# Attention backward beside a gated MLP: the order of work where the MLP phase gives way to attention, and the last output tile in two parts

## The chip, the cores and the metric

The kernel runs on one core of a Trainium2 chip. Time is device time in microseconds of that core; lower is better. The core has five instruction queues: PE (TensorE, matrix products, with its weight loads shown apart as PEld), DVE (VectorE), ACT (ScalarE), POOL (GpSimd) and SP (SyncE, which here only issues DMAs). Each queue runs its instructions in the order in which they stand; between queues there are semaphores. An instruction that waits holds up everything behind it in its queue. PE writes only to PSUM, an accumulation memory of eight banks; ACT and DVE copy from there to SBUF.

## The reference

Two branches on the same 2048 x 512 input are mixed by a gate, and the kernel returns the output and the gradients of everything but one input (eight results).

```
g = sigmoid((x * gate_w).sum(-1))
a = attention(x @ wqkv) @ wo          # 32 heads of 16, causal window of 256
b = ((gate > 0) * gate * up) @ W_down # gate = x @ W_gate, up = x @ W_up, width 1376
out = g * a + (1 - g) * b
grads = vjp(out)(grad_out)            # dx, dwqkv, dwo, dW_gate, dW_up, dW_down, dgate_w
```

## The kernel before

There are three stages.

**MLP stage (0 to about 240 us).** A loop over `n` walks 44 steps (11 slices of the MLP width by 4 groups of 512 tokens, `N1 = 44`) with 8 more iterations to drain. In iteration `n` step `n` makes gate and up, step `n-2` makes dh, step `n-3` turns and stores its results by DMA (`turn_dgu`, `keep`), and step `n-6` adds its weight gradients (`weights`) into two PSUM tiles, `wg` (two banks) and `dd` (one bank). After each fourth step these are copied to SBUF by `evac`: half of `wg` on ACT, `dd` on ACT, the other half of `wg` on DVE. The weight gradients of the last slice are not made here but later, as `tail_parts`, among the attention work. All PSUM tiles of this stage (three of tag `mm`, two of tag `tr`, `wg`, `dd`: eight banks) come from one pool, `ps1`.

From iteration `N1-2` on, the same loop also runs `project_parts(*groups[0])`, the first projections of attention. This is a list of eleven parts: two halves of Q, two of dO, two of K, the transposition of K (`tr_kv`), two halves of V, the transposition of V, and `tr_rows` (a DMA transposition of Q and dO). Two parts run per iteration, three in `N1+1`, so all eleven are done before attention begins. The second half of K and of V also makes `K1` and `V1`, copies masked for odd heads (`odd`).

**Attention stage (about 240 to 690 us).** All order is written out by hand (`tc.manual_schedule`). Work goes by turns. In turn `i` the scores S of turn `i` are made (`products`, PSUM tag `S`, one buffer of two banks), ACT takes their exponential (`front`), POOL masks it (`mask`), the products D = dO V of turn `i-1` are made (tag `D`, one buffer of two banks), and DVE multiplies them (`gradp`). Then come row sums (`rowsum`, tile BA), gradients of K and V (`cd_piece`, tile CD), and `flip`: a unit's 128 x 128 blocks are transposed either on PE (8 transpositions into a `tr` tile and one copy on ACT or DVE) two turns after its scores, or by one DMA transposition on SP one turn after them (`u.dma`). Each turn has two units, `x` = 0 and 1. The unit `x` = 0 goes by DMA in nearly all turns with two blocks; the first three turns of the first chunk, `k < 3` at `c = 0`, `q = 0`, are excepted. What PE makes in spare time is the background list `bg`: projections of the next token group, then `tail_parts`. Each part has a price. Each turn a credit grows by (sum of prices left) / (turns left), and parts run while the credit covers half of the next part's price; a part that ends a PSUM tile closes it, and at most one such part runs per turn. Background tiles and flips share the two buffers of tag `tr`.

The attention pools `ps` (tags `S`, `tr`, `D`; left side of PSUM) and `psr` (BA, CD; right side) are opened when `ps1` closes. The copies out of PSUM are dealt to ACT or DVE by `share`, which keeps a running cost of each. Flipped units lie in pool `P2`, which is opened in turn 2 in place of the last MLP tiles, or, for the edge units, in one of four `wide` buffers that the stage before used for `grad_out` and for `h_end`.

**Output stage (about 690 us to the end).** Here the compiler's list scheduler orders each queue. For each of 16 token tiles `t` PE makes `bps` (MLP output, 11 products), `aps` (attention output, 4), the `wo` gradient of the tile before (`add_dwo`, 4) and `dxps` (34 products of 512 columns, lines 1118 and 1144, with the gate-weight gradient `add_dgw` between). ACT makes `da_b` = g times grad_out (line 1085, input of `add_dwo`), and from `aps` the copies `a_sb` and `ga` (1090, 1092). DVE makes `o_sb`, `amb`, `dz` and finally `dx_sb` (1150), which a DMA stores (1152).

Of the kernel before, what the change touches and what calls it, by code (L numbers as in the profile page):

```python
# [9 lines left out]
ALU = mybir.AluOpType  # L10
# [12 lines left out]
def kernel(  # L23
# [107 lines left out]
    if True:  # L131
# [4 lines left out]
        def project_parts(c, tg):  # L136
# [15 lines left out]
            def mm(nm, which, eng):  # L152
                mm_part(nm, which, range(DC // 2, DC))
                pp = acc4[nm]
                if nm in ("Q", "dO"):
                    if nm == "Q":
                        t4["z"] = pjA.tile([P, 2, TGW], BF, tag="zT", bufs=2, name="zT")
                    dst = t4["z"][:, ("Q", "dO").index(nm), :]
                else:
                    dst = pj.tile([P, TGW], BF, tag=f"{nm}0", name=f"{nm}0")[:]  # L160
                share(dst, pp[:], TGW, by=scale if nm == "Q" else None)
                t4[nm] = dst
                if nm in ("K", "V"):
                    def odd():
                        t4[f"{nm}1"] = pj.tile([P, TGW], BF, tag=f"{nm}1", name=f"{nm}1")[:]
                        share(t4[f"{nm}1"], dst, TGW, by=par[:, 1:2], sbuf=True)

                    if pools["now"][0] is pools["first"]:
                        odd()
                    else:  # L170
                        ev.setdefault(turn + 1, []).append(("dve", odd))
# [32 lines left out]
    with ExitStack() as p1, tc.manual_schedule():  # L204
        ps1 = p1.enter_context(tc.tile_pool(name="ps1", bufs=1, space=PSUM))
        ap1 = p1.enter_context(tc.tile_pool(name="acts", bufs=1))
        db_T = rows_tile("db_T")[:].rearrange("p t a n -> p (t a n)").rearrange("p (c s) -> p c s", c=DC)
# [179 lines left out]
        def weights(k):  # L387
            if k.tg == 0:
                acc["w"] = ps1.tile([P, DC, 2 * P], F32, tag="wg", bufs=1, name="wps")
                acc["d"] = ps1.tile([P, D], F32, tag="dd", bufs=1, name="dps")  # L390
            for i in range(TPG):
# [23 lines left out]
        pools["now"] = (ps1, "tr", 2)  # L415
        pools["first"] = ps1
        first = []
        turn_x(0)
        stores = {}
        for n in range(N1 + 8):  # L420
# [17 lines left out]
            for lag, end in ((3, False), (3, True)):  # L438
                if at(lag) and (at(lag).fc == FC - 1) == end:
                    turn_dgu(at(lag))  # L440
                    keep(at(lag))
            if at(6) and at(6).fc < FC - 1:
                f = weights(at(6))
                if f is not None:
                    stores[n + 1] = f
# [12 lines left out]
            if n == N1 - 2:  # L458
                first = project_parts(*groups[0])
            for _ in range({N1 + 1: 3}.get(n, 2)):  # L460
                if first:
                    first.pop(0)[1]()
            z = n - DA0 - NT - 2
# [5 lines left out]
    if True:  # L469
# [3 lines left out]
        pps = ExitStack()  # L473
        ps = pps.enter_context(tc.tile_pool(name="attps", bufs=2, space=PSUM))
        psr = p3b.enter_context(tc.tile_pool(name="attpr", bufs=1, space=PSUM, side="right"))
        pools["now"] = (ps, "tr", 2)
# [88 lines left out]
        def grad_parts(c, seam=False):  # L565
# [3 lines left out]
            def piece(part, t0, first, last):  # L569
                if first and seam:  # L570
                    tag = "SD"[part // 2]
                    if tag not in hold:
                        hold[tag] = ps.tile([P, 2, 4, P], F32, tag=tag, bufs=1, name="wps")
                    hold[part] = hold[tag][:, part % 2, 0:3, :]
                elif first:
                    hold[part] = ps.tile([P, 3, P], F32, tag="tr", bufs=2, name="wps")[:]
                wps = hold[part]
                for t in range(t0, t0 + step):
                    nc.tensor.matmul(wps, lhsT=x_r[:, t, part * P:(part + 1) * P], rhs=sts[c][:, t, 0:3, :],  # L579
                                     start=first and t == t0, stop=last and t == t0 + step - 1)  # L580
# [61 lines left out]
        for c in range(DC):  # L642
# [6 lines left out]
            for q in range(0, NT, 2):  # L649
# [5 lines left out]
                for k, (blocks, g) in enumerate(its):  # L655
                    two = []
                    for x in range(2):
                        u = Unit()
                        u.c, u.q, u.g, u.x, u.blocks, u.nb, u.at = c, q + k // 3, g + x, x, blocks, len(blocks), len(turns_)
                        u.edge = blocks[-1][1] == blocks[-1][0] - 2  # L660
                        u.dma = x == 0 and len(blocks) == 2 and (c > 0 or q > 0 or k >= 3) and (c < DC - 1 or q < NT - 2)
                        u.turn = u.at + (1 if u.dma else 2)
# [21 lines left out]
        def products(us, vs):  # L684
# [3 lines left out]
            if vs:  # L688
                vs[0].D = ps.tile([P, 2, 2, 2, P], F32, tag="D", bufs=1, name="D")
            for u in us:  # L690
# [60 lines left out]
        def place(u):  # L751
            if u.edge:
                if u.at not in wides:
                    wides[u.at] = wide("p2")
                p2 = wides[u.at][:, u.x if u.nb == 2 else 0, :, :, :]
            elif u.nb == 2 or u.x == 0:
                p2 = pools["p2"].tile([P, 2, 4, P], BF, tag="P2", bufs=14, name="p2")[:]
# [122 lines left out]
        with tc.manual_schedule():  # L880
# [3 lines left out]
            closed = {}  # L884
            bg = []
            jobs = tail_parts()
            ready = []
# [23 lines left out]
            def lead(us):  # L911
                c, qs, ks = us[0].c, [b[0] for b in us[0].blocks], [b[1] for b in us[0].blocks]
                return "dO" in proj.get((c, max(qs) // TPG), {}) and "V1" in proj.get((c, max(ks) // TPG), {})

# [15 lines left out]
            while turn < NI + 3 or ev or cdq or bg or sums:  # L930
# [41 lines left out]
                if vs:  # L972
                    gradp(vs)
                if turn == 2:
                    fend.close()
# [70 lines left out]
    with ExitStack() as p56:  # L1046
        x_r5 = x_r

        with ExitStack() as p6:
# [18 lines left out]
            for g in range(NG):  # L1068
# [3 lines left out]
                for tl in range(GT):  # L1072
# [11 lines left out]
                    da_b = t6.tile([P, D], BF, tag="da_b")  # L1084
                    nc.scalar.mul(da_b[:], go_g[:, tl, :], g_all[:, t:t + 1])
                    pending_wo.append((t, o_g[:, tl, :, :], da_b))
# [4 lines left out]
                    ga = t6.tile([P, D], F32, tag="ga")  # L1091
                    nc.scalar.mul(ga[:], aps[:], g_all[:, t:t + 1])
                    o_sb = t6.tile([P, D], BF, tag="o_sb")
                    nc.vector.scalar_tensor_tensor(out=o_sb[:], in0=bps[:], scalar=omg_all[:, t:t + 1], in1=ga[:],
# [17 lines left out]
                    dxps = ps6.tile([P, D], F32, tag="dxps", bufs=1)  # L1112
                    nmm = 2 * FC + C3
                    i = 0

                    def gate_up(src, wt, i):
                        for fc in range(FC):
                            nc.tensor.matmul(dxps[:], lhsT=col(src, fc, lsl), rhs=W6[(wt, fc)],  # L1118
                                             start=(i + fc == 0), stop=(i + fc == nmm - 1))
                        return i + FC  # L1120

                    i = gate_up(dgT_g, "Wg", i)
                    if t > 0:
                        i = gate_up(duT_g, "Wu", i)

# [4 lines left out]

                    if pending_dgw is not None:
                        add_dgw(*pending_dgw)
                    pending_dgw = (t, dz_bf)
                    for cc in range(C3):
                        if t == NT - 1 and cc == 3:
                            add_dgw(t, dz_bf)
                            nc.scalar.copy(dgw_sb[:, 0:DC], dgw_ps[:])
                        if t == NT - 1 and cc == C3 - 4:
                            dgw_t = psa.tile([P, P], BF, tag="aps", bufs=1, name="dgw_t")
# [3 lines left out]
                            nc.sync.dma_start(out_7.rearrange("(c p) -> c p", p=P), dgw_row[:])  # L1143
                        nc.tensor.matmul(dxps[:], lhsT=T_g[:, 4 * (cc % DC) + cc // DC, lsl], rhs=W6[("wqkv", cc)],  # L1144
                                         start=(i == 0), stop=(i == nmm - 1))
                        i += 1
                    if t == 0:
                        gate_up(duT_g, "Wu", i)
                    dx_sb = t6.tile([P, D], BF, tag="dx_sb")
                    nc.vector.scalar_tensor_tensor(out=dx_sb[:], in0=S2["gw"][:], scalar=dz[:, 2:3], in1=dxps[:],  # L1150
                                                   op0=ALU.mult, op1=ALU.add)
                    (nc.sync if t == NT - 1 else nc.gpsimd).dma_start(dx_d[tsl, :], dx_sb[:])

# [29 lines left out]
```

## Time and profile before

| | us |
|---|---|
| median of 3 runs | 882.41 (881.83 to 884.45) |
| the profiled execution | 882.34 |
| its span, first to last instruction | 880.6 |
| PE busy | 855.1 (97%) |
| DVE, POOL, ACT busy | 507.2, 478.4, 395.0 |

A row of a timeline has the start in us, the length in us, the engine, the line of the kernel, the operation, output and input tiles, shapes and a count. The bracket at its end is the time for which the engine stood idle before it, and what released it. The ends of matrix products are modelled, and each overlaps the next; the time from start to start of successive products is what PE needs for them. A row of the windows view gives for a stretch of the span its length and the busy time of PE, then (with the number of instructions) of the other engines asked for, the granted clock of TensorE, the busy share of the DMA engines and GB/s.

### The profile page before, as it was taken

What the parts mean: (1) busy time and instruction counts of PE and PEld (TensorE: products, weight loads), DVE (VectorE), ACT (ScalarE), POOL (GpSimd) and SP (SyncE); (2) the same over time, 40 slices, a digit from 0 to 9 for tenths busy, and PEclk for the clock granted to TensorE, in tenths of its full rate; (3) what the DMA queues carried; (4) which work ended last, traced back from release to release, by engine and by line L of the source; (5) the groups of instructions that cost most, each with busy time, mean ns of one, the idle gap of its engine ahead of it and who ended that gap; (6) DMA issues with size and microseconds to landing.
All of it is one profiled execution on the core that took longest, in us unless ns stands there. A gap on an engine that the chain in (4) does not pass through costs nothing. (4 is left out here: it accounts for less than half of the span.)

```text
span 880.6 us, 29350 instructions
## 1 busy us (share of the span) xinstructions
PE 855.1 (97%) x12545; PEld 555.7 (63%) x12545; DVE 507.2 (58%) x763; ACT 395.0 (45%) x569; POOL 478.4 (54%) x887
## 2 busy tenths in 40 slices
PE   7999999999989999999999999999999999999998
PEld 4556665666557877777777767777778544444443
DVE  4544542332367888887888778887786132222222
ACT  5522222222366676765667656676554211111111
POOL 1644444444347787876778767787678222222111
PEclk9999999999999999999999999999999999999999
DMA  9999999999757999799998989999999999778731
GB/s 274 237 187 194 205 211 209 203 210 204 174 103 121 155 154 153 110 140 160 179 142 112 137 161 183 158 142 152 182 216 188 243 282 235 182 183 178 185 83 49
DMA packets 440876, 153.56 MB, mean 174 GB/s; under 512 B 369352, under 2 KB 438312, under 8 KB 440744
## 3 DMA queue, kind: packets, MB, share of 16 engines
q1 hardware_dynamic: 437144, 145.51, 88.5%
q0 software_dynamic: 2016, 5.64, 1.9%
q8 instruction: 98, 1.61, 0.8%
q10 hardware_dynamic: 1584, 0.53, 0.2%
q14 instruction: 34, 0.28, 0.1%
HBM read 32.15 MB, written 36.24 MB: 78 GB/s over the span
## 5 line engine op out<-in xcount | busy, mean ns | idle before, releaser
L725 DVE TENSOR_TENSOR PP<-PP,D 128x1024 bf16<-128x1024 bf16 (+1 forms) x184 | 219.0, 1190 | 56.1 <-POOL PP L718 21.6
L708 ACT ACTIVATE PP<-S 128x1024 bf16<-128x1024 f32 (+1 forms) x184 | 185.2, 1007 | 95.9 <-PE D L675 47.3
L718 POOL TENSOR_SCALAR_AFFINE_SELECT PP<-PP 128x512 bf16<-128x512 bf16 (+1 forms) x188 | 143.3, 763 | 80.2 <-ACT PP L708 77.6
L74 DVE COPY p<-pt 128x1024 bf16<-128x1024 bf16 x164 | 112.3, 685 | 10.9 <-PE pt L779 10.9
L355 POOL TENSOR_TENSOR hgu<-rg,upm 128x512 bf16<-128x512 bf16 x44 | 50.8, 1155 | 120.7 <-DVE upm L353 103.5
L779 PE MATMUL pt<-ident,PP 128*128 128x128 bf16 x1512 | 113.9, 218 | 0.1
L742 PE MATMUL BA<-KV,PP 128*128 128x33 bf16 x1440 | 106.6, 180 | 2.1 <-ACT BAs L72 1.6
L742 PEld LDWEIGHTS <-PP 128*128 128x128 bf16 x1440 | 85.7, 96 | 31.2 <-issue 11.9
L744 PE MATMUL BA<-KV,PP 128*128 128x17 bf16 x1440 | 102.4, 170 | 0.0
L395 PE MATMUL wps<-hgu_r,x_r 128*128 128x256 bf16 x640 | 96.0, 273 | 0.0
L493 PE MATMUL CD<-rq,p 128*128 128x32 bf16 x1440 | 94.8, 176 | 0.0
L496 PE MATMUL CD<-rq,p 128*128 128x16 bf16 x1440 | 93.6, 169 | 0.0
L744 PEld LDWEIGHTS <-PP 128*128 128x128 bf16 x1440 | 84.6, 96 | 10.7 <-issue 7.3
L779 PEld LDWEIGHTS <-PP 128*128 128x128 bf16 x1512 | 86.1, 97 | 0.2 <-issue 0.2
L493 PEld LDWEIGHTS <-p 128*128 128x128 bf16 x1440 | 80.7, 95 | 0.3
L496 PEld LDWEIGHTS <-p 128*128 128x128 bf16 x1440 | 80.5, 96 | 0.3
L395 PEld LDWEIGHTS <-x_r 128*128 128x128 bf16 x640 | 62.6, 98 | 28.6
L675 PE MATMUL S<-zT,K 32*128 32x128 bf16 (+3 forms) x1056 | 77.2, 238 | 1.5 <-ACT PP L708 0.7
L675 PE MATMUL D<-zT,V 32*128 32x128 bf16 (+3 forms) x1056 | 72.2, 237 | 4.6 <-DVE PP L725 4.0
L353 DVE SCALAR_TENSOR_TENSOR upm<-rg,ups 128x512 bf16<-128x512 bf16 x44 | 30.2, 687 | 80.3 <-PE ups L340 58.8
L1090 ACT COPY a_sb<-aps 128x512 f32<-128x512 f32 x16 | 9.3, 583 | 131.0 <-issue 106.5
L363 POOL TENSOR_TENSOR hgu<-dh_sb,rg 128x512 bf16<-128x512 bf16 x44 | 58.7, 1334 | 9.0 <-ACT dh_sb L361 9.0
(147 smaller groups left out, 1514.3 us busy)
## 6 DMA issues: line engine op xcount, KB each, us to landing
hgu_d<-hgu SPq DMA_DIRECT2D x44, 384.0 KB, 3.4
dqkvo_d<-rows_st SPq DMA_DIRECT2D x14, 512.0 KB, 3.8
duT_g<-hgu_d SPq DMA_DIRECT2D x8, 640.0 KB, 5.3
gt<-hgu_d SPq DMA_DIRECT2D x7, 640.0 KB, 5.6
dgT_g<-hgu_d SPq DMA_DIRECT2D x7, 640.0 KB, 5.0
p<-PP SPq DMA_TRANSPOSE x171, 4.0
out_dram<-wst SPq DMA_DIRECT2D x20, 128.0 KB, 2.9
go_in<-in_grad_out_dram SPq DMA_DIRECT2D x4, 512.0 KB, 9.4
```

What stands on the lines that cost most here:

```text
L74: nc.vector.tensor_copy(out, in_)
L363: nc.gpsimd.tensor_tensor(out=k.hgu[:, 2, :], in0=dh_sb[:], in1=k.rg[:], op=ALU.mult)
L395: nc.tensor.matmul(acc["w"][:, c, :], lhsT=x_r[:, t, c * P:(c + 1) * P], rhs=k.dgu_r[:, :, i, :], start=(go_ and c % 2 == 0), stop=no_, sk ...
L493: nc.tensor.matmul(cd[0][:, h, :], lhsT=p2[:, 0, pr, :], rhs=rq[:, h, 0:2 * Dh], start=cd[1], stop=True, skip_group_check=True)
L496: nc.tensor.matmul(cd[0][:, h, 0:Dh], lhsT=p2[:, 1, pr, :], rhs=rq[:, h, 2 * Dh:3 * Dh], start=False, stop=True, skip_group_check=True)
L675: nc.tensor.matmul(dst, lhsT=proj[(u.c, kb // TPG)][nm + ("", "1")[par]][rows[par], (kb % TPG) * P:(kb % TPG + 1) * P], rhs=proj[(u.c, qb ...
L708: nc.scalar.activation(two[:].rearrange("p x a b q -> p x a (b q)")[:, :, 0, 0:n], flat(us[0].S[:], n), ACT.Exp)
L718: nc.gpsimd.affine_select(out=out, in_=out, compare_op=ALU.is_ge, fill=0.0, base=0 if up else -1, pattern=[[0, 2], [0, b1 - b0], [1 if up ...
L725: nc.vector.tensor_tensor(out=v(1), in0=v(0), in1=flat(vs[0].D[:], n), op=ALU.mult)
L742: nc.tensor.matmul(BA[:, h, 0:33], lhsT=u.PP[:, 0, 2 * i + pr, :], rhs=kv[:, kb % TPG, h, 1:34], start=(first and pr == 0), stop=True, ski ...
L744: nc.tensor.matmul(BA[:, h, 33:50], lhsT=u.PP[:, 1, 2 * i + pr, :], rhs=kv[:, kb % TPG, h, 0:17], start=False, stop=True, skip_group_check ...
L779: nc.tensor.transpose(pt[:, a, b if u.nb == 2 else 2 * u.x + b, :], u.PP[:, a, b, :], ident[:])
```

## The change

1. The MLP stage's `wg` and `dd` go to a pool of their own, `psw`, on the right side of PSUM. `D` goes to a pool of its own, `psd`, beside `ps`.
2. In the MLP loop, iteration `N1-2`, `N1-1` and `N1` run the two parts of Q, dO and K; `N1` also runs `tr_rows`, and `N1+1` runs K's transposition, ahead of `weights`. V's three parts are kept in a list `behind`. Turn 0 of attention starts when `K1` is there: it makes the first scores, then V's two parts, then two parts from the background list, apart from those that the credit allows. Turn 1 makes V's transposition behind its scores, products and `gradp`.
3. The units `x` = 0 of the first two turns are flipped by DMA too, into a `wide` buffer, since `P2` isn't open yet.
4. `da_b` is written behind `a_sb` and `ga`, except in the last tile.
5. In the last tile `dxps` is made in two parts: 34 products of 384 columns, then 34 of 128 columns into a tile of tag `bps`; each part has its own DVE operation and store. The work on the gate-weight gradient stays in the first part.

```diff
+        psw = p1.enter_context(tc.tile_pool(name="psw", bufs=1, space=PSUM, side="right"))
...
-                acc["w"] = ps1.tile([P, DC, 2 * P], F32, tag="wg", bufs=1, name="wps")
-                acc["d"] = ps1.tile([P, D], F32, tag="dd", bufs=1, name="dps")
+                acc["w"] = psw.tile([P, DC, 2 * P], F32, tag="wg", bufs=1, name="wps")
+                acc["d"] = psw.tile([P, D], F32, tag="dd", bufs=1, name="dps")
...
+            if n == N1 + 1:
+                first.pop(0)[1]()
             if at(6) and at(6).fc < FC - 1:
                 f = weights(at(6))
...
-            for _ in range({N1 + 1: 3}.get(n, 2)):
-                if first:
-                    first.pop(0)[1]()
+            for _ in range({N1 - 2: 2, N1 - 1: 2, N1: 2}.get(n, 0)):
+                first.pop(0)[1]()
+            if n == N1:
+                first.pop()[1]()
...
+        psd = pps.enter_context(tc.tile_pool(name="attpd", bufs=1, space=PSUM))
...
-                        u.dma = x == 0 and len(blocks) == 2 and (c > 0 or q > 0 or k >= 3) and (c < DC - 1 or q < NT - 2)
+                        u.dma = x == 0 and len(blocks) == 2 and (c < DC - 1 or q < NT - 2)
...
-                vs[0].D = ps.tile([P, 2, 2, 2, P], F32, tag="D", bufs=1, name="D")
+                vs[0].D = psd.tile([P, 2, 2, 2, P], F32, tag="D", bufs=1, name="D")
...
+            elif u.at < 2 and u.x == 0:
+                if "p2" not in wides:
+                    wides["p2"] = wide("p2")
+                p2 = wides["p2"][:, u.at, :, :, :]
...
+            behind = [f[1] for f in first]
...
-                return "dO" in proj.get((c, max(qs) // TPG), {}) and "V1" in proj.get((c, max(ks) // TPG), {})
+                return "dO" in proj.get((c, max(qs) // TPG), {}) and ("K1" if turn == 0 else "V1") in proj.get((c, max(ks) // TPG), {})
...
                 if vs:
                     gradp(vs)
+                if turn == 0:
+                    behind.pop(0)()
+                    behind.pop(0)()
+                    background()
+                    background()
+                elif behind:
+                    behind.pop(0)()
...
-                    nc.scalar.mul(da_b[:], go_g[:, tl, :], g_all[:, t:t + 1])
+                    if t == NT - 1:
+                        nc.scalar.mul(da_b[:], go_g[:, tl, :], g_all[:, t:t + 1])
...
                     nc.scalar.mul(ga[:], aps[:], g_all[:, t:t + 1])
+                    if t < NT - 1:
+                        nc.scalar.mul(da_b[:], go_g[:, tl, :], g_all[:, t:t + 1])
...
+                    def dx_part(dxps, n0, n1, pending):
+                        count = [0]
+
+                        def product(w, key):
+                            nc.tensor.matmul(dxps[:, n0:n1], lhsT=w, rhs=W6[key][:, n0:n1], start=(count[0] == 0), stop=(count[0] == nmm - 1))
+                            count[0] += 1
...
+                        nc.vector.scalar_tensor_tensor(out=dx_sb[:, n0:n1], in0=S2["gw"][:, n0:n1], scalar=dz[:, 2:3], in1=dxps[:, n0:n1],
+                                                       op0=ALU.mult, op1=ALU.add)
+                        (nc.sync if t == NT - 1 else nc.gpsimd).dma_start(dx_d[tsl, n0:n1], dx_sb[:, n0:n1])
+
                     dx_sb = t6.tile([P, D], BF, tag="dx_sb")
...
+                    cut = D if t < NT - 1 else D - P
+                    dx_part(ps6.tile([P, D], F32, tag="dxps", bufs=1, name="dxps"), 0, cut, pending_dgw)
+                    if cut < D:
+                        dx_part(psa.tile([P, D], F32, tag="bps", bufs=1, name="dxps_end"), cut, D, None)
+                    pending_dgw = (t, dz_bf)
```

More of the change, by code (lines that the diff above doesn't have):

```diff
@@ L166, in odd @@
                         share(t4[f"{nm}1"], dst, TGW, by=par[:, 1:2], sbuf=True)
-                    if pools["now"][0] is pools["first"]:
+                    if (c, tg) == groups[0]:
                         odd()
@@ L415 @@
         pools["now"] = (ps1, "tr", 2)
-        pools["first"] = ps1
         first = []
@@ L572, in piece @@
                     if tag not in hold:
-                        hold[tag] = ps.tile([P, 2, 4, P], F32, tag=tag, bufs=1, name="wps")
+                        hold[tag] = (ps if tag == "S" else psd).tile([P, 2, 4, P], F32, tag=tag, bufs=1, name="wps")
                     hold[part] = hold[tag][:, part % 2, 0:3, :]
@@ L1111 @@
                             nc.sync.dma_start(out_3[c * P:(c + 1) * P, :], ws[:])
-                    dxps = ps6.tile([P, D], F32, tag="dxps", bufs=1)
                     nmm = 2 * FC + C3
[L1114 to L1124, printed above, removed]
                     def add_dgw(t_, dz_):
@@ L1129, in add_dgw, with gate_col_grad @@
                                              start=(t_ == 0 and c == 0), stop=(t_ == NT - 1), skip_group_check=True)
[L1131 to L1135, printed above, removed]
+                    def gate_col_grad(cc):
+                        if cc == 3:
                             add_dgw(t, dz_bf)
                             nc.scalar.copy(dgw_sb[:, 0:DC], dgw_ps[:])
-                        if t == NT - 1 and cc == C3 - 4:
+                        if cc == C3 - 4:
                             dgw_t = psa.tile([P, P], BF, tag="aps", bufs=1, name="dgw_t")
@@ L1143 @@
                             nc.sync.dma_start(out_7.rearrange("(c p) -> c p", p=P), dgw_row[:])
[L1144 to L1148, printed above, removed]
-                    dx_sb = t6.tile([P, D], BF, tag="dx_sb")
-                    nc.vector.scalar_tensor_tensor(out=dx_sb[:], in0=S2["gw"][:], scalar=dz[:, 2:3], in1=dxps[:],
-                                                   op0=ALU.mult, op1=ALU.add)
@@ L1152, with gate_up @@
-                    (nc.sync if t == NT - 1 else nc.gpsimd).dma_start(dx_d[tsl, :], dx_sb[:])
+                    def dx_part(dxps, n0, n1, pending):
[3 more added lines that the diff above has]
+                            count[0] += 1
+                        def gate_up(src, wt):
+                            for fc in range(FC):
+                                product(col(src, fc, lsl), (wt, fc))
+                        gate_up(dgT_g, "Wg")
+                        if t > 0:
+                            gate_up(duT_g, "Wu")
+                        if pending is not None:
+                            add_dgw(*pending)
+                        for cc in range(C3):
+                            if t == NT - 1 and n0 == 0:
+                                gate_col_grad(cc)
+                            product(T_g[:, 4 * (cc % DC) + cc // DC, lsl], ("wqkv", cc))
+                        if t == 0:
+                            gate_up(duT_g, "Wu")
+                        nc.vector.scalar_tensor_tensor(out=dx_sb[:, n0:n1], in0=S2["gw"][:, n0:n1], scalar=dz[:, 2:3], in1=dxps[:, n0:n1],
+                                                       op0=ALU.mult, op1=ALU.add)
+                        (nc.sync if t == NT - 1 else nc.gpsimd).dma_start(dx_d[tsl, n0:n1], dx_sb[:, n0:n1])
```

## The prediction

> **What bounds the kernel now.** After the page's shares I read the view of busy time by stretches of the span, with the seam between MLP and attention cut out, and then the timelines there, PE's first.
>
> ```profile
> 300.00:400.00 100.00, 97.11 (x2361) 74.19 (x2360) 85.07 (x123) 67.97 (x93) 79.76 (x180) 1.00 0.98 142
> ...
> 712.00:870.00 158.00, 158.00 (x780) 72.33 (x778) 42.27 (x94) 25.98 (x44) 30.34 (x40) 1.00 0.71 173
> ...
> sum 20.00, PE 15.98; mean PE 2.66
> ```
>
> PE is the bound: it works 97.11 of 100 us in attention and 158 of 158 in the output stage. The last row is the sum over 237 to 257 us, the seam: PE works 15.98 of 20.00 us and idles 4.02. Only there can work be put into holes. What is won there should stay won: attention runs PE at 97% behind it, and every later event hangs on the turns.
>
> ```profile
> 239.67 0.39 PE L187 MATMUL ptp<-ident,K 128*128 128x128 bf16 x4
> 239.90 1.03 PE L149 MATMUL pp<-x,p 128*128 128x512 bf16 x4
> 241.60 0.40 PE L187 MATMUL ptp<-ident,V 128*128 128x128 bf16 x4 [0.68 <-ACT V L72]
> 242.51 0.39 PE L675 MATMUL S<-zT,K 16*128 16x256 bf16 x4 [0.52 <-DVE KV L74]
> ...
> 244.14 0.28 PE L675 MATMUL S<-zT,K 16*128 16x256 bf16 x2 [0.27 <-ACT PP L708]
> ...
> 246.12 0.28 PE L675 MATMUL D<-zT,V 16*128 16x256 bf16 x2 [0.24 <-DVE PP L725]
> ...
> 246.67 1.05 PE L779 MATMUL pt<-ident,PP 128*128 128x128 bf16 x16
> 248.50 1.02 PE L149 MATMUL pp<-x,p 128*128 128x512 bf16 x4 [0.78 <-DVE p L74]
> ...
> 251.78 0.38 PE L187 MATMUL ptp<-ident,K 128*128 128x128 bf16 x4 [0.73 <-DVE p L74]
> ...
> 255.90 0.28 PE L675 MATMUL S<-zT,K 16*128 16x256 bf16 x2 [0.28 <-ACT PP L708]
> 256.57 0.23 PE L675 MATMUL D<-zT,V 16*128 16x128 bf16 x2 [0.38 <-DVE PP L725]
> ```
>
> The brackets name the holes. V's transposition waits 0.68 for ACT's copy of V; the first scores wait 0.52 for the copy of that transposition, the last reader of `ps1`; the flips of turns 2 and 3 take 16 transpositions each (246.67, and the same ahead of 251.78), so both `tr` buffers, and the next projection waits 0.78 and 0.73 for one. The brackets sum to 3.88, nearly the 4.02.
>
> **The change, part by part.** *Scores ahead of V, pools of their own.* What stands on the other queues:
>
> ```profile
> 240.14 0.59 ACT L72 CAST dst<-dps 128x512 bf16<-128x512 f32 x1
> 240.96 0.59 ACT L72 CAST V<-pp 128x512 bf16<-128x512 f32 x1 [0.23 <-PE pp L149]
> 243.07 1.02 ACT L708 ACTIVATE PP<-S 128x1024 bf16<-128x1024 f32 x1 [1.52 <-PE S L675]
> ```
> ```profile
> 240.88 0.51 DVE L90 TENSOR_SCALAR KV<-ptp 128x512 bf16<-128x512 bf16 x1
> ...
> 244.85 1.22 DVE L725 TENSOR_TENSOR PP<-PP,D 128x1024 bf16<-128x1024 bf16 x1 [2.39 <-POOL PP L718]
> ...
> 247.76 0.69 DVE L74 COPY p<-pt 128x1024 bf16<-128x1024 bf16 x1
> ```
> ```profile
> 237.97 1.39 POOL L363 TENSOR_TENSOR hgu<-dh_sb,rg 128x512 bf16<-128x512 bf16 x1 [2.95 <-ACT dh_sb L361]
> ...
> 239.36 0.31 POOL L183 MEMSET KV<- 128x32 bf16 x1
> 244.17 0.65 POOL L718 TENSOR_SCALAR_AFFINE_SELECT PP<-PP 128x512 bf16<-128x512 bf16 x1 [4.49 <-ACT PP L708]
> ```
>
> K's transposition moves ahead of the last weight products, which then end at 239.90 (0.23 later, as the K row and the next start). The first scores can start there instead of at 242.51, since S no longer shares a pool with the copies of `wg` and `dd`. But K's copy into KV must be done first, as the last reader of `ps1`. It writes the tile of POOL's memset, which ends at 239.67 behind L363; if the copy waits for that, it ends at 239.67 + 0.51 and the scores start at 240.2. So 239.9 to 240.2; I take 240.2, because DVE's copy is the kind of wait that the bracket of 0.52 shows. ACT then takes the exponential behind `dst` at about 240.9 instead of 243.07. Behind the scores PE has V, Q of the next group, and dO by the credit (at turn 0 about 9.0 of prices over 11 turns, 0.82, against 0.43 for the first half of a projection): three projections of 0.86 (four products of 512 columns; 0.216 each, worked out with the tail), where it stood still. That third one needs the `tr` buffer of V, so ACT's copy of V, which now stands behind the exponential: 240.9 + 0.92 + 0.59 = 242.4, when PE, at 242.2, waits 0.2. Turn 1 starts near 243.3 instead of 244.14, with dO (0.86) done ahead: 1.7 us ahead. Queued behind the waiting things: dO's copy stands on DVE ahead of the first `gradp`, which starts at 244.1 instead of 244.85, so turn 2 waits for its end at 245.3 (0.3), and turn 3 for the second one (K's copy 0.69, then 1.22, done at 247.4) about 0.8; turn 5 waits 0.6 in the same way. New holes: 0.3 + 0.2 + 0.3 + 0.8 + 0.6 = 2.2, and by the same rows no more than the old 4.02.
>
> *First flips by DMA.* Eight of the 16 transpositions in each of turns 2 and 3 leave PE, and with them one copy per turn leaves DVE or ACT. How long 16 take, and eight products of 384 columns, is in the chain, where it runs without a break; the third row is of the 13 flips by DMA between 250 and 285.
>
> ```profile
> 669.90 0.91 PE pt L779 x16
> 676.92 1.30 PE wps L579 x8
> ```
> ```profile
> DMA to landing us min/median/max: 3.0/3.8/4.9
> ```
>
> Sixteen take 0.91 on PE: that is removed. With 8 per turn one `tr` buffer stays free, so the two holes of 0.78 and 0.73 go, by what the turns with one such flip show, none of which is named in the brackets between 252 and 255; they are among the 4.02. The two DMAs stand on SP, issued from 245.3 and 247.5. Flips of this kind land within 4.9 us, by 252.4. SP's stores of the MLP stage lie ahead of them, and `tr_rows` leaves that place for one ahead of the last `turn_dgu`; it delays that by its issue of about 1.3 us (the row of it below), which only the background work from 255 on needs. The readers of the flips come in turn 6.
>
> ```profile
> 243.23 1.28 SPq L175 DMA_TRANSPOSE rows<-zT  x1
> ...
> 257.12 0.18 PE L493 MATMUL CD<-rq,p 128*128 128x32 bf16 x1
> ```
>
> Before, they start at 257.12; some 3 us earlier that is 254, still 1.7 behind the landing. Cost 0; if the cover went, at most 0.5 by a late landing in a busy stretch.
>
> *Sum at the seam.* Holes of 4.02 plus 0.91 of work removed, less the 2.2 of new holes: 2.7. The ends are 4.02 + 0.91 = 4.9 (no new hole) and 0.4 (new holes as long as the old ones plus the 0.5). I take 2.8, a little above the sum, since two of the new holes overlap copies that the shorter flips bring forward.
>
> *`da_b` behind `a_sb` and `ga`.*
>
> ```profile
> 857.48 0.72 ACT L1085 ACTIVATE da_b<-gt,g_all 128x512 bf16<-128x512 bf16 x1
> 867.95 0.59 ACT L1090 COPY a_sb<-aps 128x512 f32<-128x512 f32 x1 [9.75 <-issue]
> ```
>
> ACT is idle 9.75 us per tile, and the scheduler already puts the next tile's `da_b` behind this tile's `ga`. Its reader, `add_dwo`, comes a tile later. I take 0; the ends are a gain of some tenths in the first tile, where ACT's `da_b` waits for the load of `grad_out`, and the loss of the second rival.
>
> *Last `dx` in two parts.*
>
> ```profile
> 869.60 4.75 PE dxps L1118 x22
> ...
> 877.23 0.75 DVE dx_sb L1150
> ```
> ```profile
> 705.82 0.15 DVE L1102 TENSOR_TENSOR dz<-g_all,omg_all 128x1 f32<-128x1 f32 x1
> ```
> ```profile
> out_dram<-dx_sb SPq DMA_DIRECT2D x1, 128.0 KB, 1.7
> ```
> ```profile
> out_dram<-wst SPq DMA_DIRECT2D x2, 128.0 KB, 2.8
> out_dram<-dst SPq DMA_DIRECT2D x1, 128.0 KB, 2.6
> ```
>
> 34 products of 512 columns at 0.216 (4.75 / 22) take 7.3. Of 384 columns they take 0.1625 (1.30 / 8), of 128 columns 0.057 (0.91 / 16): 34 x 0.2195 = 7.46, so PE ends 0.1 later. DVE's last operation falls from 0.75 for 512 columns towards 0.15 for one: 0.15 + 0.60/4 = 0.30, so 0.45 less. The last store has 32 KB instead of 128; how much of its 1.7 is fixed no row shows, so 0 to 0.4, and I take 0.2. The first part's DVE operation (about 0.6) and store lie beside the second part's 1.94 of PE. Sum 0.45 + 0.2 - 0.1 = 0.55, ends 0.1 and 0.8. The Trainium skill, "DMA: Bandwidth & Descriptors", Specifications, speaks against this: it gives 512 B as the least transfer at full rate, with a read-modify-write below, and the second store has rows of 256 B. In this trace the stores of `wst`, with such rows, take 2.8 us to land and that of `dst`, of as many bytes in 1 KB rows, 2.6, so the trace agrees in direction and shows little of it; by the page the 0.2 would go and the sum here be about 0.35.
>
> ```profile
> span 880.6 us, 29350 instructions
> ```
>
> **Total.** 2.8 + 0.55 = 3.3, of the profiled execution's 882.34 (span 880.6 and 1.7 around it). That lies within 0.1 of the median, so I carry it over: 882.4 - 3.3 = 879.1.
>
> **The rivals.** *A: the new holes cost more.* DVE sets the pace of turns 1 to 5: `gradp` 1.22, a flip copy 0.69 and a projection's cast 0.69 stand in one queue, and turns are closer. If two more waits as long as those it removes appear (0.78 + 0.73), the gain is 3.3 - 1.5 = 1.8: 880.6. For it speaks that D waits for DVE twice already; against it that DVE has 2.39 of idle time ahead of its first `gradp`.
>
> *B: slower, by `da_b`.* If the scheduler places `add_dwo` of a tile where its `da_b` isn't done, PE waits for 0.72 in each of 15 tiles: 10.8 us, so 882.4 - 3.3 + 10.8 = 889.9. It decides the sign from 0.22 per tile on. Against it: the 9.75 of idle time on ACT; for it: PE has no slack in that stage (158 of 158), so any wait there counts fifteen times.
>
> *C: won at the seam and lost again before the output stage.*
>
> ```profile
> 690.00:707.00 17.00, 14.97 (x70) 1.00 1.09 240
> ```
> ```profile
> 700.08 0.52 POOL L527 MEMSET d<- 32x512 bf16 x1 [11.79 <-DMA d<-in_B_W_up_dram]
> ```
>
> There PE idles 2 us, and its release comes from POOL's memset, which waits for a DMA, with DMA engines full (1.09). If that DMA doesn't come earlier, the 2.8 is lost and the tail's 0.55 stays: 881.9. Against it: the loads are issued by events of the last turns, so they move along.
>
> **How the numbers follow.** The forecast 0.57, A 0.19, C 0.10, B or another slowdown 0.14. A change under 0.3% (2.65 us) can hardly be told from none here. Faster by more means below 879.76: most of the forecast's own range, 877.0 to 880.2, and a small part of A: 0.56. Within: C, most of A: 0.30. Slower: 0.14. The low end is the seam's 4.9 plus the tail's 0.55, 877.0. The high end must pass A and C and leave out B: 882.8, no gain at all and 0.4 for the scatter of the runs.
>
> **What would show it.** Right: in the profile after, scores at 240 us, idle PE of about 2 in the 20 us from 237, 16 fewer L779, the last DVE operation near 0.3 us, and no idle PE from tile to tile in the output stage. Wrong: a bracket at the first scores beyond 1 us; D waiting for `gradp` in most turns to 257; CD waiting for the DMA flips; the first output tile starting no earlier than 686 to 690; an idle time at `wo_ps`.

## The result, and the profile after

| | before | after |
|---|---|---|
| median, us | 882.93 (7 runs, 881.83 to 884.45) | 879.87 (7 runs, 878.61 to 881.28) |
| ratio | | 0.9964, 95% interval 0.9952 to 0.9975 |
| the profiled execution | 882.34 | 881.28 |
| its span | 880.6 | 879.6 |

The changed kernel is 3.06 us faster; 3.3 were forecast, and a time of 879.1. The two profiled executions differ by only 1.06 us, and the profile after is of the slowest of its seven runs. So a reader who takes the difference of the two spans for the effect of the change is misled by 2 us. Where those 2 us went can be found in the trace.

PE's timeline of the changed kernel at the seam (row sums and a few products left out):

```profile
236.20 0.39 PE L187 MATMUL ptp<-ident,K 128*128 128x128 bf16 x4
...
239.13 0.39 PE L679 MATMUL S<-zT,K 16*128 16x256 bf16 x4
239.46 1.90 PE L149 MATMUL pp<-x,p 128*128 128x512 bf16 x8
241.55 1.02 PE L149 MATMUL pp<-d,p 128*128 128x512 bf16 x4 [0.19 <-ACT V L72]
242.51 0.28 PE L679 MATMUL S<-zT,K 16*128 16x256 bf16 x2
...
245.03 0.61 PE L787 MATMUL pt<-ident,PP 128*128 128x128 bf16 x8
245.47 0.39 PE L187 MATMUL ptp<-ident,K 128*128 128x128 bf16 x4
245.79 0.28 PE L679 MATMUL S<-zT,K 16*128 16x256 bf16 x2
246.68 0.23 PE L679 MATMUL D<-zT,V 16*128 16x128 bf16 x2 [0.61 <-DVE PP L729]
...
250.78 0.28 PE L679 MATMUL D<-zT,V 16*128 16x256 bf16 x2 [0.29 <-DVE PP L729]
...
260.23 0.82 PE L624 MATMUL wps<-dgu_end,x_r 128*128 128x192 bf16 x8 [0.58 <-DVE p L74]
```

The first scores follow the last weight products without a bracket; V, Q and dO stand in a row behind them; eight transpositions are followed by K's transposition without a wait. Holes of 0.19, 0.61 and 0.29 are left, and one of 0.58 at 260.23. The whole execution was already 0.86 us earlier at the end of the MLP stage, which belongs to its first 35 us and not to the change (over all profiles this mark lies between 227.69 and 229.57, in old and new kernels mixed), so times of the two profiles are better compared as distances between marks. Four marks that each kernel has once: the start of the last `hgu` on POOL (end of the MLP stage), of the fourth and the last `rinv` on DVE (attention under way, attention's end), and of the fourth `dz` on DVE (output stage under way). In the changed kernel:

```profile
227.69 1.15 POOL L356 TENSOR_TENSOR hgu<-rg,upm 128x512 bf16<-128x512 bf16 x1 [3.62 <-DVE upm L354]
```
```profile
270.73 0.19 DVE L803 RECIPROCAL rinv<-BAs 128x8 f32<-128x8 f32 x1
...
673.86 0.19 DVE L803 RECIPROCAL rinv<-BAs 128x8 f32<-128x8 f32 x1
...
732.68 0.69 DVE L1120 TENSOR_REDUCE dz<-amb 128x1 f32<-128x512 f32 x1 [1.46 <-POOL amb L1118]
```

and in the kernel before:

```profile
228.55 1.15 POOL L355 TENSOR_TENSOR hgu<-rg,upm 128x512 bf16<-128x512 bf16 x1 [3.62 <-DVE upm L353]
```
```profile
274.69 0.19 DVE L795 RECIPROCAL rinv<-BAs 128x8 f32<-128x8 f32 x1
...
677.56 0.19 DVE L795 RECIPROCAL rinv<-BAs 128x8 f32<-128x8 f32 x1
...
733.50 0.69 DVE L1101 TENSOR_REDUCE dz<-amb 128x1 f32<-128x512 f32 x1 [1.46 <-POOL amb L1099]
```

The seam (first to second mark) takes 43.04 instead of 46.14 us: 3.10 won. Attention takes 403.13 instead of 402.87. The start of the output stage takes 58.82 instead of 55.94: 2.88 lost in this execution. The view of waits of the changed kernel between 660 and 714 us (who waited for whom; us in total, times, longest) names the place:

```profile
PE dxps L1153 <- DMA d<-in_B_W_up_dram: 1.9, 1, 1.9
PE dxps L1153 <- POOL d L531: 0.9, 1, 0.9
PE dxps L1153 <- DVE dx_sb L1171: 0.2, 1, 0.2
```

PE waits for a load of W_up, then for the memset behind it, and TensorE's clock drops as well (below). Rival C of the prediction had named this place. Whether the change causes it is what the experiments had to decide.

### The profile page after: what moved, and what is told of

The parts are those of the page before. It is cut to its first block, busy times and chain, and to the rows that moved or that the text cites. A ratio compares the mean times of both kernels' runs of the same rounds, so it can differ in the third digit from the quotient of the medians.

```text
span 879.6 us, 29392 instructions
## 1 busy us (share of the span) xinstructions
PE 856.6 (97%) x12563; PEld 557.2 (63%) x12563; DVE 507.9 (58%) x764; ACT 393.5 (45%) x567; POOL 478.5 (54%) x887
```

## The experiments

The same four marks in every profile, in us between them, with the lead at the seam over 46.14:

| kernel | seam | lead | attention | output start |
|---|---|---|---|---|
| before | 46.14 | | 402.87 | 55.94 |
| last dx in two parts alone | 46.14 | 0 | 402.95 | 58.60 |
| `da_b` moved alone | 46.15 | 0 | 403.07 | 57.27 |
| before, late memset | 46.64 | | 403.48 | 55.89 |
| changed, first profile | 43.04 | 3.10 | 403.13 | 58.82 |
| changed, second | 43.05 | 3.09 | 403.19 | 56.43 |
| changed, third | 43.04 | 3.10 | 403.10 | 56.97 |
| parts 1 to 3 alone | 43.04 | 3.10 | 403.20 | 57.10 |
| without first flips by DMA | 44.62 | 1.52 | 403.11 | 56.35 |
| without own pools | 43.99 | 2.15 | 403.08 | 57.38 |
| changed, late memset | 43.04 | 3.10 | 403.31 | 55.56 |
| the same again | 43.04 | 3.10 | 403.10 | 56.97 |
| early W_up | 43.03 | 3.11 | 410.89 | 54.14 |
| early W_up, late memset | 43.04 | 3.10 | 407.23 | 54.84 |

Apart from one outlier (46.64) the seam repeats within 0.02 us, so one profile is enough there for a difference well above that outlier's 0.5. In the outlier TensorE's clock dropped at the seam (the last section has the row); its edit stands 440 us later. The start of the output stage doesn't repeat: kernels with the old seam and the memset where it was show 55.94 to 58.60 (mean 57.27), those with the new seam 56.35 to 58.82 (mean 57.18).

**The changed kernel again.** No edit.

> The changed kernel once more, unchanged. Theory S (the seam's gain of 3.1 us reaches the last tiles; what its first profile lost between 682 and 712 us is chance of one execution): the median is 2.6 to 3.6 us under before, and this profile keeps 2 us or more of the lead of 3.7 to 3.9 us behind 712. Theory C (the load of W_up's transposition does not come earlier, so the lead is always lost there): again under 1 us of lead behind 712, and the median gain stays near 1 us.

Median 880.23 against 883.38: ratio 0.9962 (0.9945 to 0.9978). The lead at the seam is 3.09. Behind 712 us this execution stands 2.9 ahead of the one before, 0.6 of which it had from its first 35 us. A third set, taken later beside another kernel:

> The changed kernel, for the comparison with the late memset. Theory S: 2.6 to 3.6 us under the kernel before, for the third time; in its profile the lead at 275 us beyond that at the end of the MLP stage is 3.1 again, and what is left of it at 712 us lies between 0 and 3.

Ratio 0.9949 (0.9935 to 0.9962), lead 3.10, output start 56.97. By the medians that is 4.1 us, more than the 2.6 to 3.6 expected: the changed kernel is where it was (879.63), and the kernel before is slower in this set (883.75). Theory C falls: the lead is not always lost, and the old kernels show the same scatter.

**The parts alone.** The seam alone keeps the old `da_b` and

```diff
-                    cut = D if t < NT - 1 else D - P
+                    cut = D
```

> Parts 1 to 3 of the change (scores ahead, pools, first flips by DMA); da_b and the last dx as before. Theory S: the seam carries the gain, 2.4 to 3.3 us faster than before, lead of about 3.1 us (beyond any difference at the start) from 270 us on. Rival T (the tail carries it): under 1 us.

Ratio 0.9971 (0.9959 to 0.9984), 2.6 us of 883.4 (3.1 by the medians), lead 3.10: the seam carries nearly all.

The other two are the kernel before with that part of the change's diff alone.

> Part 5 alone (last dx in two parts). By the prediction 0.55 us faster (0.1 to 0.8): last DVE operation 0.35 instead of 0.75, PE 0.1 later, store 0.2 shorter. By the first profile of the changed kernel 0.2. Rival T: over 1.5 us.

> Part 4 alone (da_b behind a_sb and ga). Theory: no difference, within 0.5 us of before, since ACT idles 9.7 us per tile. Rival B: 0.7 us per tile lost at the wo products, 10 us slower. Rival G: a_sb and ga of tile 0 no longer wait for the load of grad_out, some tenths faster.

The dx in two parts alone gives 1.0002 (0.9990 to 1.0015), `da_b` alone 0.9996 (0.9983 to 1.0008): neither can be told from nothing. For the last tile the profiles say more than the medians. DVE's last operations and the end, in the profile of the two-part dx alone:

```profile
877.53 0.61 DVE L1152 SCALAR_TENSOR_TENSOR dx_sb<-gw_b,dz,dxps 128x384 bf16<-128x384 bf16 x1 [1.90 <-PE dxps L1134]
879.43 0.35 DVE L1152 SCALAR_TENSOR_TENSOR dx_sb<-gw_b,dz,dxps_end 128x128 bf16<-128x128 bf16 x1 [1.29 <-PE dxps_end L1134]
```
```profile
out_dram<-dx_sb SPq DMA_DIRECT2D x1, 96.0 KB, 1.6
out_dram<-dx_sb SPq DMA_DIRECT2D x1, 32.0 KB, 1.4
```

From the last tile's `dz` to the end of the span, four profiles with one part take 8.63 to 8.96 (mean 8.72), ten with two parts 8.35 to 8.52 (mean 8.43): 0.29 won, or 0.21 without the one of 8.96. DVE's operation fell from 0.75 to 0.35 and PE's products took 0.09 more, as forecast. The last store lands 1.4 us after its issue here, and 1.4 or 1.5 in the other nine, instead of 1.7 in the four with the whole store. But the span ends no sooner for it: from the end of DVE's operation to the end of the span it is 2.62, 2.62, 2.65 and 2.96 in one part and 2.65 to 2.82 in two. What lies between the landing and the end of the span is in no view.

**What carries the seam.** The two kernels of this part ran once each, so only their profiles are used. First the old condition for the flips again:

```diff
-                        u.dma = x == 0 and len(blocks) == 2 and (c < DC - 1 or q < NT - 2)
+                        u.dma = x == 0 and len(blocks) == 2 and (c > 0 or q > 0 or k >= 3) and (c < DC - 1 or q < NT - 2)
```

> The changed kernel with part 3 undone: the units x = 0 of the first two turns are flipped on PE again. Measured as the lead over the kernel before at the row sums (rinv), less the difference already there at the end of the MLP stage. By the prediction part 3 brings 0.91 of PE work and the two waits of 0.78 and 0.73, so the lead at 270 us falls from 3.1 to about 0.7. Rival: with scores and projections spread otherwise the waits for tr do not come back, and only the 0.9 goes: a lead of 2.2.

The waits of PE between 236 and 262 us in that kernel:

```profile
PE ptp L187 <- ACT p L72: 0.7, 1, 0.7
PE D L679 <- DVE PP L729: 0.4, 1, 0.4
PE pp L149 <- DVE p L74: 0.3, 1, 0.3
PE pp L149 <- ACT V L72: 0.2, 1, 0.2
```

The lead is 1.52, between the two expectations: the flips are worth 1.58. The waits for a `tr` buffer do come back, as 0.70 and 0.34 instead of 0.78 and 0.73; with the 0.91 of transpositions that would be 1.95, and the waits for `gradp` become 0.46 shorter (0.44 instead of 0.61 and 0.29), which leaves 1.5.

Then the pools, both put back at once:

```diff
-                acc["w"] = psw.tile([P, DC, 2 * P], F32, tag="wg", bufs=1, name="wps")
-                acc["d"] = psw.tile([P, D], F32, tag="dd", bufs=1, name="dps")
+                acc["w"] = ps1.tile([P, DC, 2 * P], F32, tag="wg", bufs=1, name="wps")
+                acc["d"] = ps1.tile([P, D], F32, tag="dd", bufs=1, name="dps")
...
-                vs[0].D = psd.tile([P, 2, 2, 2, P], F32, tag="D", bufs=1, name="D")
+                vs[0].D = ps.tile([P, 2, 2, 2, P], F32, tag="D", bufs=1, name="D")
```

> The changed kernel with the PSUM pools put back (wg and dd in ps1, D in ps), order and flips as changed. By the prediction the first scores then wait for the copies of wg and dd (ACT and DVE, done about 1.4 us after the last weight product), so S starts 1.2 to 1.5 us later and the lead at 270 us is about 1.8 instead of 3.1. Rival: the order alone carries it, the lead stays at 2.9 or more.

```profile
240.63 0.39 PE L677 MATMUL S<-zT,K 16*128 16x256 bf16 x4 [1.19 <-DVE wst L74]
```

The scores wait 1.19 for DVE's copy of the weight gradients, as expected; 0.95 of it is left in the lead, since the 0.2 of waiting for V's copy then goes. So of the 3.10 the flips carry about half (1.58), the pools a third (0.95); what is left by subtraction, 0.57, would be the order's if the parts simply added up; it wasn't run alone.

**The start of the output stage.** The order of POOL's queue there, in the second profile of the changed kernel:

```profile
697.17 0.52 POOL L531 MEMSET d<- 32x512 bf16 x1 [12.26 <-DMA d<-in_B_W_up_dram]
697.63 2.92 POOL L590 DMA_DIRECT2D out_dram<-ws  x4
700.05 1.05 POOL L1115 DMA_DIRECT2D out_dram<-o_sb  x1
700.62 1.67 POOL L1118 TENSOR_TENSOR amb<-amb,go_g 128x512 f32<-128x512 f32 x1
```

A memset of half a microsecond stands 12.26 us at the head of the queue, waiting for a load; behind it four stores whose data has long been there, and behind these `amb`, on which PE's second `dxps` hangs. So:

```diff
-            clear("Wu")
             for f in S2["grads"]:
                 store = f()
                 if store is not None:
                     store()
+            clear("Wu")
```

> The changed kernel with the memset of W_up's last rows on POOL moved behind the stores of the last wqkv gradients. Theory C1 (POOL's queue behind the memset is what PE waits for at the second output tile): the four stores, 2.9 us, leave the path, amb of tile 0 comes 2.9 us earlier after the memset, and the median falls by up to 2 us (the wait at the second dx). Rival C2 (the DMA of W_up's rows itself is the wait): PE still waits for it in the first dx, and the median stays within 0.7 us of the changed kernel.

Five runs gave 878.67, ratio 0.9940 (0.9928 to 0.9953). PE's waits between 676 and 714 us, in its profile:

```profile
PE dxps L1153 <- POOL d L531: 1.0, 1, 1.0
PE dxps L1153 <- DMA d<-in_B_W_up_dram: 0.4, 1, 0.4
```

The wait of 1.9 for the second dx (`dxps` for DVE's `dx_sb`), which the profile before and the second and third of the changed kernel have, is gone, as C1 says; what is left is the load itself, as C2 says. Once more, beside the changed kernel on the same chip:

> The changed kernel with the late memset again, beside the changed kernel itself in the next run on the same chip. If its gain of the first time (five runs: 878.67 against some 880.2) is real, 1.2 to 2.2 us under the changed kernel again. If it was the luck of those five runs, as the gain of only 0.4 us in the kernel before suggests, within 0.7 us of it.

Median 878.28 against 879.63, ratios 0.9942 (0.9926 to 0.9958) and 0.9949 (0.9935 to 0.9962) to the kernel before. The intervals overlap: faster than the changed kernel by 0.6 us (ratios) or 1.4 (medians) in this set, not proved. In this profile, of the slowest of the six runs, the wait for `dx_sb` is gone too, but PE waits 2.8 us in all for the load and the memset of W_up, and the output stage's start takes as long as in the changed kernel beside it (56.97). The kernel before with the same edit:

> The kernel before with only the memset of W_up's last rows moved behind the stores. If the wait behind the memset is there in both kernels (1.91 us in the profile before), this is 1 to 2 us faster than before, and the gain adds to that of the change. Rival: the change made that wait, by coming to it earlier, and here the time stays within 0.5 us of before.

Ratio 0.9986 (0.9973 to 0.9999), which is 1.2 us, but 0.4 by the medians: its twelve runs fall into two groups, five from 879.9 to 881.5 and seven from 883.0 to 885.7. The wait of 1.9 is in the old kernel too and goes here as well; whether that is worth 0.4 or 1.2 us these runs don't settle. This edit on the changed kernel gave the lowest medians of all.

Taking the load out of the way altogether, into the last chunk of attention, where late loads then go every second turn from token tile 8 on instead of 12:

```diff
+                14: turns("Wu", B_W_up, 4, 8, "x2") + turns("Wu", B_W_up, 8, 12, "d2") + [lambda: clear("Wu")],
...
-            for f in turns("Wu", B_W_up, 4, 8, "x2") + turns("Wu", B_W_up, 8, 12, "d2"):
-                f()
-            clear("Wu")
...
-                if late and (late[0] is not load_wo or turn > NI) and (not us or turn % (4 if us[0].c == DC - 1 and us[0].q < 12 else 2) == 1):
+                if late and (late[0] is not load_wo or turn > NI) and (not us or turn % (4 if us[0].c == DC - 1 and us[0].q < 8 else 2) == 1):
```

> The changed kernel with W_up's last four transposing loads and their memset moved from the start of the output stage into the list of late loads of the last chunk of attention, where their buffers are free; late loads then go every second turn from token tile 8 on instead of 12. If the load of W_up is what the output stage's start waits for (C2), the waits between 682 and 712 us go and the kernel is 1.5 to 4 us faster than the changed one, with less scatter. Rival: the DMA engines are full in the last attention turns too, flips land late there, and what is won at 700 is lost before 680 (lead at 677 us falls under 3).

Ratio 1.0001 (0.9991 to 1.0011): the whole gain is gone. The output start is the shortest of all (54.14), and attention takes 7.8 us more. POOL between 640 and 684 us, and then the waits of all engines in that stretch:

```profile
648.68 1.09 POOL L723 TENSOR_SCALAR_AFFINE_SELECT PP<-PP 128x1024 bf16<-128x1024 bf16 x1 [1.69 <-ACT PP L713]
656.16 0.51 POOL L531 MEMSET d<- 32x512 bf16 x1 [6.38 <-DMA d<-in_B_W_up_dram]
```
```profile
DVE PP L730 <- POOL PP L723: 7.5, 5, 6.1
POOL d L531 <- DMA d<-in_B_W_up_dram: 6.4, 1, 6.4
PE D L680 <- DVE PP L730: 5.8, 1, 5.8
```

It is the same memset again: it waits 6.38 us for its load, the masks stand behind it, `gradp` behind the masks, PE behind `gradp`. With the memset moved behind the stores:

> As the kernel with the early loads of W_up, but its memset on POOL stands behind the stores of the last wqkv gradients, not among the masks of attention. Theory M (the loss between 640 and 680 us there was the memset: it waited 6.4 us for its DMA at the head of POOL's queue, masks and gradp behind it): no wait of 5.8 us, a lead of about 3.1 at 677 us kept to 712, and a time of 877 to 878.5, up to 1.4 us under the kernel with the late memset alone, since the wait for W_up in the first dx goes too. Rival D (the DMA engines are what is short): flips land late between 640 and 680, CD or gradp wait, and the time is that of the kernel with the late memset or more.

The wait of 5.8 is gone, as theory M says. But the time is 882.26, ratio 0.9994 (0.9983 to 1.0006): at the `rinv` of 657.71 this execution is still 3.2 us ahead of the one before (0.6 of it from the first 35 us), and at the last one, 678.23, it is 0.7 behind. A wait that this profile adds there:

```profile
ACT PP L713 <- DMA p<-PP: 5.4, 4, 2.0
```

ACT's exponential waits four times for a buffer whose flip by DMA hasn't landed. The changed kernel's profiles have no such wait, so rival D holds in that the flips are late, and about 4 us are lost for 2 won. Its cause is not shown: the DMA engines' mean share from 660 to 684 us is 1.10 here and 1.07 in the first profile of the changed kernel, the moved loads also stand in SP's queue between the flips, and the kernel before with the late memset, which moved no load, has two such waits (2.4 us) at 665 to 669.

## Why the prediction was right

- **The total** was forecast at 3.3 and measured at 3.06 (879.1 against 879.87). From the table and the tail: 3.10 at the seam, less 0.17 in attention (mean of the three old kernels without the late memset 402.96, of the six new ones 403.13), 0.1 at the output start (means, far inside its scatter), 0.2 to 0.3 in the last tile: 3.2 to 3.3. The seam gave 0.3 more than forecast and the last tile about 0.3 less; that the total was met is partly luck. Of the 0.8 between 879.1 and 879.87, 0.5 is the starting point: 882.4 was the median of three runs, that of seven is 882.93.
- **The seam** was forecast at 2.8 and measured at 3.10. PE from the first mark to the second, before and then changed:

```profile
228.55:274.69 46.14, 41.93 (x634) 1.00 0.67 124
```
```profile
227.69:270.73 43.04, 40.91 (x617) 1.00 0.81 142
```

  PE idles 2.13 us instead of 4.21 and works 1.02 us less: 2.08 + 1.02 = 3.10. So the forecast's terms come out near in sum (4.02 of holes removed, 0.91 of work, 2.2 of new holes), but not each new hole in its place. In the 20 us from 237 the changed PE idles 1.35 us, where about 2 were forecast (first row below). Of the five new holes, the first scores' 0.3 did not come: DVE's copy into KV ran at 237.41, ahead of POOL's memset of that tile at 238.51 (the other rows), so the dependency that I held possible isn't there. dO's 0.2 came as 0.19; turn 2's 0.3 left no bracket; turn 3's 0.8 came as 0.61 and turn 5's 0.6 as 0.29. A hole of 0.58 at 260.23 I had not seen: one background part is done earlier, and the next needs a `tr` buffer behind DVE's flip copy; I take that from the order, no run tests it.

```profile
237.00:257.00 20.00, 18.65 (x264) 1.00 0.84 142
```
```profile
237.41 0.51 DVE L90 TENSOR_SCALAR KV<-ptp 128x512 bf16<-128x512 bf16 x1
```
```profile
238.51 0.31 POOL L183 MEMSET KV<- 128x32 bf16 x1
```

- **The first flips by DMA** were put at 0.91 of work and 1.51 of holes, 2.42 in all; undoing them costs 1.58, since without them the waits for `gradp`, which the prediction counted as new holes, are shorter. This term and that one overlap, so neither stands alone at the size it has in the sum. The flips did land in time: no CD product waits for them.
- **The last dx** was the mis-sized term: 0.55 forecast, 0.2 to 0.3 measured. The DVE part (0.45; measured 0.40) and PE's 0.1 were right; the failed step is "I take 0.2" for the smaller store. It does land 0.2 to 0.3 sooner after its issue, but that doesn't shorten the time: the span ends 2.65 to 2.82 behind DVE's operation, where three of the four with the whole store have 2.62 to 2.65. The prediction took it that what the landing wins the execution wins; what stands between the two stays open. The Trainium skill, "DMA: Bandwidth & Descriptors", Specifications, had spoken against the 0.2 with its least size of 512 B for full rate; the runs agree that the 0.2 doesn't come, but not that the store lands no sooner, so they don't bear out the row size as the reason.
- **`da_b`**: 0 forecast, nothing measured. The scheduler runs it as before: in the changed profile the first two `da_b` still stand ahead of the first `a_sb`.

```profile
693.41 1.33 ACT L1111 ACTIVATE da_b<-go_g,g_all 128x512 bf16<-128x512 bf16 x2 [6.88 <-DMA go_g<-in_grad_out_dram]
694.65 0.56 ACT L1107 COPY a_sb<-aps 128x512 f32<-128x512 f32 x1
```

- **The rivals.** A (more holes) fell: 1.35 us of idle time in the 20 us, and 2.13 between the marks, where it needed some 3.7 (2.2 and 1.5). B fell: 156 of 156 us busy from 712 to 868. C named the right place and the wrong cause: up to 2.9 us are lost there in single executions, but in old and new kernels alike. That the profile before was a good pass through that place (55.94 of a range to 58.60) and the profile after the worst was chance. The prediction's sum stood on work hidden or not within one profile, and it took no account of how far that stretch scatters.

## What to carry to other kernels

When a stage ends and the next begins, ask which tile the next stage's first product waits for: a pool that holds both the tiles finished last and the place for the next stage's first tile makes the first product wait for the last copy; separating them was worth 0.95 of 3.10 us here. A short instruction that waits for a load, put in the queue of a busy engine, holds everything behind it: PE waited 1.9 us behind the half-microsecond memset in one place and 5.8 in another. Such a wait is not yet a gain: moved out of the way, it brought some 1 us (not proved) in the first place and 1.4 by the medians in the second, with other waits left in both. Compare two profiles by distances between marks that both have, not by their spans: here the marks repeated within 0.02 us at the seam (all profiles but one), while the spans hid two thirds of the gain.

## What the runs showed of the hardware

TensorE's granted clock dropped in the first profile of the changed kernel, on one busy core, after short gaps. PE by stretches:

```profile
696.00:699.00 3.00, 0.96 (x4) 1.00 0.90 131
699.00:702.00 3.00, 2.17 (x6) 0.64 1.23 264
702.00:705.00 3.00, 3.00 (x13) 0.79 1.26 310
```

```profile
698.31 0.59 PE L1153 MATMUL dxps<-d,duT_g 128*128 128x512 bf16 x2 [1.94 <-DMA d<-in_B_W_up_dram]
699.83 0.58 PE L1153 MATMUL dxps<-d,duT_g 128*128 128x512 bf16 x1 [0.93 <-POOL d L531]
700.21 1.91 PE L1094 MATMUL bps<-x,f 128*128 128x512 bf16 x4
701.92 1.69 PE L1094 MATMUL bps<-d,f 128*128 128x512 bf16 x4
703.45 0.81 PE L1094 MATMUL bps<-p,f 128*128 128x512 bf16 x3
704.09 1.03 PE L1098 MATMUL aps<-wo_z,early 128*128 128x512 bf16 x4
```

The gaps were 1.94 and 0.93 us with two products between them. The eleven products of `bps` behind them took 3.88 us, from 700.21 to 704.09, where eleven of 0.216 take 2.37: waits of 2.9 us cost 1.5 more. The Trainium skill, "TensorE: Matmul & The Clock Gate", Part 1, names an idle window of about 3.4 us ahead of the slow state; here no unbroken idle time came near that, only a stretch of 3.6 us (696.2 to 699.8) in which PE worked 0.4. In the second profile gaps of 0.61 and 1.92, six microseconds apart, left the clock at 1.00.

It also dropped once at the old seam, in the profile of the kernel before with the late memset. Until then PE had no longer wait at the seam than 0.68 us; from 244 to 246 us the clock was 0.68, and then:

```profile
246.00:248.00 2.00, 2.00 (x24) 0.50 0.18 34
```

The 16 transpositions in this stretch take 1.30 us instead of 1.05, and the seam 0.5 more: this is the outlier of the table. The other three profiles with the old seam have the same holes and no such loss, so the holes alone don't decide it; what does, these runs don't show.

The start of the output stage takes 55.9 to 58.8 us in kernels with the same order of work there. The load of W_up lands at different times, and nothing in these runs says why; that stays open.
